# A hand-written order of operations anew: eight chunks of a fused attention and feed-forward kernel

## The chip, the cores and the metric

The kernel runs on 1 core of a Trainium2 chip. The metric is the device time of one execution in microseconds (us), the median of several runs; lower is better.

## The reference

A linear attention (softmax of q over the head's elements, softmax of k over the sequence), and a feed-forward layer with SiLU on its result:

```python
# q, k, v: (8 batches, 8 heads, 576 positions, 64), float32
q_s = softmax(q, axis=-1)                       # over the 64 elements
k_s = softmax(k, axis=2)                        # over the 576 positions
kv  = einsum('bhsd,bhse->bhde', k_s, v)
x   = einsum('bhsd,bhde->bhse', q_s, kv)        # then (4608 tokens, 512)
h   = x @ w_in                                  # (4608, 2048)
out = (h * sigmoid(h)) @ w_out                  # (4608, 512), float32
```

## The kernel before

The 4608 tokens are worked in nine chunks of 512: chunk 0 to chunk 8. Attention is worked per batch (576 positions); its results feed the chunk that holds its tokens. Chunk 0 is done in another form than the rest, with 576 tokens at once ("wide"), and chunk 1 has the 448 tokens that are left of its 512.

The whole program is straight-line. Each piece of work is an operation with a short name, and a string ORDER lists the names; a loop at the end calls them one by one. Each engine (PE, DVE, ACT, POOL, and SP for its DMA orders) executes its own operations in the order in which they stand in that string; between engines there are only semaphores, set from the data and buffers that operations share. So the string fixes five queues, and an operation that has to wait holds up all that stands behind it on its engine. The first operations of batch 0 (loads, softmax, its products, and the first two products of chunk 0) stand ahead of ORDER as plain calls.

The names, as far as the text needs them (b is a batch, c a half of its heads, t a chunk):

- `lqb.c`, `lkb.c`, `lvb.c`: a load of q, k or v (L152), 576 KB. Batches 1 and 2 are loaded from POOL's queue, batches 0 and 3 to 7 from SP's. Each of q, k, v has two buffers, so a load waits until the operation that read the older content is done: `eqb.c` (ACT, Exp of q, L163), `ekb.c` (ACT, Exp of k, L168), `vcb.c` (cast of v). `W1a0` to `W1d` and `W2a` to `W2d` load the weights (L564, L570) from POOL's queue.
- `zb.c` sums the Exp of q (DVE), `nb.c` divides by it (POOL, L216; for batches 0 and half of 1 on DVE). `tqb` is a transpose of q by DMA from SP's queue (L226); for batches 0 and 1 `trb.c` transposes on PE and `tcb.ca`, `tcb.cb` copy the result (ACT, DVE). `kvb` is the product of k and v (PE, L248), `kcb` normalises it (DVE). `Xt.i` (PE, L282; `xt1.i` for chunk 1) makes a chunk's x, `xt.ca` and `xt.cv` copy it from PSUM (ACT or DVE).
- Chunk 0: `wF` is block F of 16 of its first product (PE, L307: 8 matmuls of 128x288, four contraction steps for each of two PSUM banks), `hF` the tanh (ACT, L320), `vF` the rest of SiLU (DVE, L323), `pF` step F of 16 of the second product (PE, L445, four matmuls of 512 columns into PSUM banks 2 to 5). The blocks F use four sets of two banks in turn (4, 2, 0, 6). `po0` to `po3` copy its output, `os0` to `os3` store it.
- Chunks 1 to 8, first product: one level of a seven-product scheme (Strassen-Winograd). `gt.g.i` is product i (PE, L425, 8 matmuls) for half g of the hidden columns, in the order 1 2 6 5 7 4 3, accumulated in two pairs of banks. `st.g.i` copies a partial sum from PSUM (ACT or DVE), `at.g.i` adds another (DVE, L403), `ut.g.i` is SiLU (ACT, L409). `xst.i` and `WSg.i` are the sums of operands (DVE). Half of chunk 1 is done plainly: `m0` to `m7` (PE, L335, banks 0 to 3 in turn), `mu0` to `mu7` its SiLU (ACT, L345).
- Chunks 1 to 8, second product: `bt.i.m` (PE, L503, 8 matmuls; `e` for chunk 8) in the same scheme, with `St.i` and `T1` to `T4` as operand sums (DVE), `sat`, `sbt`, `sct` as partial sums (ACT), `wat`, `wbt`, `wct`, `wlt` as output sums, `ot.m` as stores (SP). The second product of a chunk runs between the first-product steps of the next.
- `gcopy` (ACT) copies 64 tokens' columns of chunk 0's hidden values over to chunk 1. `heat` is PE work without a result.

Exp and SiLU need different function tables on ACT; a change of table is an instruction of its own (ACT_TABLE_LOAD, 1.28 us).

Of the kernel before, what the change touches and what calls it, by code (L numbers as in the profile page):

```python
# [15 lines left out]


ORDER = """
    lk1.0 w1 lk1.1 w2 h1 w0 h2 v1 w3 h0 W2b1 w5 v0 v2 h3 w4 WS0.1 h5 w6 v3 h4 W2b2 v4 w7 v5 w8 h7 h6 v7 w9
    lv1.0 h8 v6 w11 v8 h9 lv1.1 w10 eq1.0.0 v9 h11 WS0.2 w12 eq1.1.0 v11 h10 w13 WS1.1 eq1.0.1 v10 h12 w15  # L20
    qp1a h13 v12 w14 eq1.1.1 v13 qp1b WS1.2 W2c1 p0 h14 z1.0 ek1.0 p1 z1.1.0 n1.0 z1.1.1 p2 h15 ek1.1 v15 p3
    WS1.4 W2c2 tr1.0 v14 lq2.0 p4 tc1.0a tc1.0b lq2.1 n1.1 p5 W2d p6 lk2.0 T1 vc1.0 lk2.1 p7 tr1.1 lv2.0
    vc1.1a vc1.1b gcopy WS1.3 kv1 lv2.1 tc1.1b p8 tc1.1a kc1 WS0.3 xt1.0 xt1.1 x1.0a x1.1v p9 x1.2a x1.3v
    g1.1.1 xs1.1 xs1.2 xs1.4 g1.1.2 s1.1.0a WS0.4 p10 xs1.3 eq2.0 a1.1.0 p11 eq2.1 z2.0 g1.1.6 g1.1.5
    s1.1.1a z2.1 n2.0 p12 ek2.0 g1.1.7 p13 s1.1.2v n2.1 ek2.1 p14 a1.1.2 g1.1.4 p15 tq2 u1.1.4 g1.1.3 po2v
    vc2.1 po1a m0 po3v po0a a1.1.1 u1.1.0 vc2.0 m1 lk3.0 mu0 m2 T2 lq3.0 mu1 lq3.1 m3 u1.1.2 lk3.1 T3 m4
    lv3.0 u1.1.1 lv3.1 m5 T4 mu2 os0 mu4 kv2 mu5 m6 mu3 kc2 X2.0 mu6 X2.1 x2.0v m7 x2.1a x2.3a x2.2v g2.1.1
    mu7 xs2.1 xs2.2 g2.1.2 s2.1.0v b1.1.0 ek3.0 S1.1 g2.1.6 eq3.1 lk4.0 S1.2 b1.2.0 os1 s2.1.1a b1.1.1 xs2.3
    xs2.4 eq3.0 a2.1.0 g2.1.7 vc3.0 sa1 b1.2.1 lq4.0 z3.1 s2.1.2a g2.1.5 vc3.1 ek3.1 b1.6.0 a2.1.2 n3.1
    lk4.1 g2.1.4 z3.0 g2.1.3 u2.1.0 g2.0.2 u2.1.4 wa1 n3.0 b1.6.1 a2.1.1 u2.1.2 g2.0.1 sb1 S1.3 kv3 tq3  # L30
    s2.0.0a b1.5.0 kc3 u2.1.1 S1.4 g2.0.6 b1.7.0 s2.0.1v lv4.0 ek4.1 b1.7.1 lv4.1 a2.0.0 os3 g2.0.7 sc1
    ek4.0 b1.5.1 s2.0.2v g2.0.5 eq4.0 lk5.0 wc1 lq4.1 g2.0.4 a2.0.2 os2 b1.4.0 vc4.0 lk5.1 z4.0 u2.0.4
    g2.0.3 u2.0.2 b1.3.0 lv5.0 vc4.1 a2.0.1 u2.0.0 lq5.0 b1.4.1 n4.0 X3.0 wl1v X3.1 kv4 x3.0a x3.1v x3.2a
    b1.3.1 kc4 x3.3a xs3.1 u2.0.1 g3.1.1 xs3.2 wb1 g3.1.2 s3.1.0a xs3.3 xs3.4 g3.0.2 S2.1 g3.1.6 S2.2 eq4.1
    b2.2.0 s3.1.1a b2.1.0 z4.1 ek5.0 b2.1.1 a3.1.0 g3.1.7 n4.1 sa2 ek5.1 b2.6.0 s3.1.2v g3.1.5 vc5.0 tq4
    g3.1.4 a3.1.2 u3.1.0 b2.6.1 u3.1.4 S2.3 g3.1.3 sb2 lq5.1 g3.0.1 u3.1.2 a3.1.1 lv5.1 lk6.0 b2.7.0 s3.0.0a
    o1.0 S2.4 b2.2.1 u3.1.1 a3.0.0 g3.0.6 lv6.0 b2.7.1 s3.0.1v eq5.0 g3.0.5 wa2 g3.0.7 sc2 lq6.0 z5.0 b2.4.0
    s3.0.2a lk6.1 b2.5.0 vc5.1 eq5.1 a3.0.2 g3.0.4 o1.1 n5.0 z5.1 g3.0.3 u3.0.4 b2.5.1 a3.0.1 n5.1 u3.0.0
    b2.4.1 wc2 u3.0.2 X4.0 X4.1 kv5 x4.1v x4.0a tq5 wl2v b2.3.0 u3.0.1 x4.3v g4.1.1 xs4.1 x4.2a b2.3.1 xs4.2
    s4.1.0a S3.1 g4.1.2 wb2 g4.1.6 lq6.1 a4.1.0 ek6.1 b3.1.0 xs4.3 s4.1.1a b3.1.1 xs4.4 S3.2 ek6.0 g4.1.5  # L40
    g4.1.7 sa3 eq6.0 b3.2.0 s4.1.2v eq6.1 b3.2.1 lq7.0 kc5 lk7.0 b3.6.0 a4.1.2 lv6.1 lq7.1 g4.1.4 o2.0 wa3
    g4.1.3 z6.0 u4.1.4 b3.5.0 u4.1.0 S3.3 g4.0.1 lk7.1 b3.6.1 a4.1.1 s4.0.0a g4.0.2 sb3 u4.1.1 g4.0.6 a4.0.0
    b3.5.1 s4.0.1a S3.4 b3.7.0 vc6.1 u4.1.2 g4.0.7 z6.1 vc6.0 g4.0.5 s4.0.2a b3.7.1 a4.0.2 n6.1 g4.0.4 sc3
    u4.0.2 g4.0.3 wc3 n6.0 b3.3.0 u4.0.4 a4.0.1 b3.4.0 u4.0.0 X5.0 X5.1 kv6 x5.0a x5.1v tq6 x5.3a x5.2v
    b3.3.1 u4.0.1 xs5.1 g5.1.1 xs5.2 wb3 b3.4.1 s5.1.0v o2.1 ek7.1 g5.1.2 kc6 g5.1.6 wl3a xs5.3 xs5.4 a5.1.0
    lv7.0 b4.2.0 s5.1.1a lv7.1 b4.1.0 S4.1 eq7.1 g5.1.7 ek7.0 b4.2.1 s5.1.2v o3.1 g5.1.5 S4.2 b4.1.1 u5.1.0
    a5.1.2 g5.1.4 sa4 g5.0.2 o3.0 u5.1.4 wa4 g5.1.3 S4.3 u5.1.2 vc7.1 g5.0.1 b4.6.0 a5.1.1 vc7.0 s5.0.0a
    b4.6.1 a5.0.0 u5.1.1 g5.0.6 S4.4 b4.5.0 s5.0.1a b4.5.1 sb4 u5.0.0 g5.0.7 g5.0.5 s5.0.2v b4.7.0 eq7.0
    a5.0.2 b4.7.1 z7.1 g5.0.4 sc4 g5.0.3 b4.4.0 a5.0.1 u5.0.4 b4.4.1 wc4 u5.0.1 X6.0 X6.1 kv7 x6.0v u5.0.2
    x6.3v b4.3.0 x6.1a kc7 b4.3.1 x6.2a xs6.1 xs6.2 g6.1.1 xs6.4 wl4v g6.1.2 S5.1 s6.1.0a b5.1.0 a6.1.0  # L50
    g6.1.6 xs6.3 g6.0.2 wb4 s6.1.1a S5.2 b5.1.1 o4.0 b5.2.0 S5.3 g6.1.7 S5.4 b5.2.1 s6.1.2a z7.0 g6.1.5 sa5
    g6.1.4 wa5 n7.0 b5.6.0 a6.1.2 u6.1.4 b5.6.1 g6.0.1 n7.1 sb5 u6.1.0 g6.1.3 s6.0.0a b5.7.0 a6.1.1 tq7
    b5.7.1 a6.0.0 u6.1.1 g6.0.6 sc5 b5.5.0 s6.0.1a o4.1 g6.0.5 u6.1.2 g6.0.7 b5.5.1 s6.0.2v b5.4.0 wc5
    g6.0.4 a6.0.2 b5.4.1 u6.0.4 b5.3.0 u6.0.2 X7.0 X7.1 x7.0a x7.1v g6.0.3 x7.2a xs7.1 u6.0.0 g7.1.1 x7.3v
    a6.0.1 b5.3.1 s7.1.0a xs7.2 g7.1.2 wl5a u6.0.1 g7.1.6 o5.1 a7.1.0 b6.1.0 s7.1.1a xs7.4 xs7.3 g7.1.5 wb5
    g7.1.7 S6.1 o5.0 b6.1.1 s7.1.2a S6.2 g7.0.2 sa6 a7.1.2 u7.1.0 g7.1.4 S6.3 b6.2.0 u7.1.4 g7.1.3 u7.1.2
    g7.0.1 a7.1.1 b6.2.1 s7.0.0a b6.6.0 wa6 u7.1.1 S6.4 g7.0.6 b6.6.1 s7.0.1v b6.5.0 sb6 a7.0.0 g7.0.7
    b6.7.0 s7.0.2a b6.7.1 b6.5.1 sc6 u7.0.0 g7.0.4 wc6 g7.0.5 u7.0.4 b6.4.0 a7.0.2 b6.3.0 X8.0 X8.1 x8.0v
    g7.0.3 x8.2a x8.1v u7.0.2 b6.4.1 xs8.1 a7.0.1 x8.3a g8.1.1 xs8.3 g8.1.2 s8.1.0a xs8.2 b6.3.1 wl6a u7.0.1
    g8.1.6 wb6 b7.1.0 S7.1 o6.0 s8.1.1a b7.2.0 a8.1.0 g8.1.7 o6.1 xs8.4 b7.1.1 S7.2 s8.1.2a g8.1.5 sa7  # L60
    u8.1.0 b7.2.1 a8.1.2 g8.1.4 S7.3 g8.1.3 u8.1.4 g8.0.2 a8.1.1 u8.1.2 g8.0.1 u8.1.1 b7.6.0 s8.0.0v b7.6.1
    wa7 g8.0.6 a8.0.0 sb7 b7.5.0 s8.0.1a S7.4 b7.7.0 g8.0.7 g8.0.5 s8.0.2v b7.7.1 a8.0.2 b7.5.1 sc7 u8.0.0
    g8.0.4 wc7 g8.0.3 u8.0.4 b7.4.0 a8.0.1 u8.0.2 b7.3.0 u8.0.1 b7.3.1 e1.0 wb7 S8.1b e1.1 o7.0 S8.1a b7.4.1
# [7 lines left out]
def kernel(  # L71
# [477 lines left out]
    for name, src in (("qt", q), ("kt", k)):  # L549
        load(0, name, src, 0, nc.sync)  # L550
        if name == "qt":
            load(0, name, src, 1, nc.sync)
    load(0, "vt", v, 0, nc.sync)
    load(0, "kt", k, 1, nc.sync)
    load(0, "vt", v, 1, nc.sync)
# [19 lines left out]
    heat(20)  # L575
    exp_q(0, 0)
    qsum(0, 0)
    exp_q(0, 1)
    nc.gpsimd.tensor_copy(gate, st[0]["kt", 0][0:1, 1, 0:1])
    load_w1(0, 4, 0, 2)  # L580
    load_w1(0, 4, 2, 4)
    load_w1(4, 8)
    load_w1(8, 12)
    load_w1(12, 16)
    load(1, "qt", q, 0, nc.gpsimd)
    load(1, "qt", q, 1, nc.gpsimd)
    load_w2(0, 4)

    qnorm(0, 0, nc.vector)
    qsum(0, 1)  # L590
    exp_k(0, 0)
    tr(0, 0, 0, 5, 0)
    tr(0, 0, 5, J, 1)
    heat(7)
    qnorm(0, 1, nc.vector)
    vcast(0, 0, nc.scalar)
    trcopy(0, 0, 0, 5, 0, nc.scalar)
    trcopy(0, 0, 5, J, 1)
    kv(0, 0)
    kvcopy(0, 0, 1)  # L600
    tr(0, 1, 0, 5, 2)
    tr(0, 1, 5, J, 3)
    exp_k(0, 1)
    xt_mm(0, 0, 0, 320, 4, 0)
    xt_mm(0, 0, 320, 256, 0, 0)
    heat(3, 6)
    vcast(0, 1, nc.scalar, 0, 1)
    vcast(0, 1, nc.vector, 1, 2)
    trcopy(0, 1, 0, 5, 2, nc.scalar)
    trcopy(0, 1, 5, J, 3)  # L610
    kv(0, 1)
    kvcopy(0, 1, 2)
    heat(2, 3)
    xt_evac(0, 0, 4, 0, 320, 0, nc.scalar)
    xt_evac(0, 0, 0, 0, 256, 320, nc.vector)
    xt_mm(0, 1, 0, 320, 6, 0)
    xt_mm(0, 1, 320, 256, 2, 0)
    wide_mm(0, (0, 1))
    xt_evac(0, 1, 6, 0, 320, 0, nc.scalar)
    xt_evac(0, 1, 2, 0, 256, 320, nc.vector)  # L620
    wide_mm(2, (0, 1))
# [217 lines left out]
```

## Time and profile before

| what | value |
|---|---|
| median of 3 runs | 257.55 us (257.51 to 258.29) |
| profiled execution, its own time | 258.61 us |
| its span | 256.6 us |
| PE busy | 249.1 us (97%), 2732 matmuls |
| DVE, ACT, POOL busy | 206.2 us (80%), 190.9 us (74%), 65.8 us (26%) |
| granted TensorE clock | 1.0 throughout |
| DMA | 45.89 MB, of it q1 (issued by SP and ACT) 33.56 MB, q0 (issued by POOL) 11.60 MB |
| chain that ended last | PE 76%, DMA 11%, issue 5%, POOL 3%, ACT 2%, DVE 1% |

The span is the time between the first and the last instruction in one profiled execution; its own time has 2.0 us more around it. The chain that ended last is followed back from the last instruction, at each step to what released it. The span is drawn in 40 slices of 6.4 us; a digit is the busy share of a slice in tenths. "L" numbers are lines of the kernel, and a line can be that of a helper that many operations share. Matmul ends are modelled, so PE counts as busy in small waits too.

### The profile page before, as it was taken

How to read it: one execution, taken by the hardware profiler on the slowest of the kernel's cores; microseconds unless marked ns; L12 is line 12 of the kernel's file. 1: busy time of each engine (PE TensorE's matmuls, PEld its weight loads, DVE VectorE, ACT ScalarE, POOL GpSimd, SP SyncE). 2: the span in 40 equal slices, each digit the busy share in tenths (PEclk: the TensorE clock that was granted, in tenths of full speed). 3: DMA queues.
4: the chain of work that ended last, by engine and by line, in shares of the span. 5: the costliest groups of instructions: out<-in, count | busy, mean ns of one | idle time of the engine just before them, and what ended most of it. 6: DMA issues, size and time to landing. Idle time of an engine off the chain costs nothing.

```text
span 256.6 us, 6459 instructions
## 1 busy us (share of the span) xinstructions
PE 249.1 (97%) x2732; PEld 204.2 (80%) x2732; DVE 206.2 (80%) x276; ACT 190.9 (74%) x225; POOL 65.8 (26%) x62
## 2 busy tenths in 40 slices
PE   8799999999999999999999999999999999999994
...
DMA  7999999979959957996874960021807000600365
GB/s 248 348 181 297 302 301 283 351 140 393 378 128 213 403 187 137 361 335 168 276 266 68 224 236 3 3 52 32 163 14 153 13 0 4 148 18 0 66 141 123
DMA packets 36044, 45.89 MB, mean 179 GB/s; under 512 B 16288, under 2 KB 21088, under 8 KB 36016
## 3 DMA queue, kind: packets, MB, share of 16 engines
q1 hardware_dynamic: 29456, 33.56, 45.5%
q0 software_dynamic: 6160, 11.60, 17.8%
...
## 4 chain that ended last, share of the span: by engine, by line
PE 76%; DMA 11%; issue 5%; POOL 3%; ACT 2%; DVE 1%; ACTq 0%; POOLq 0%
PE PS L503 37%; PE PS L425 33%; DMA qt<-in_q_dram 5%; DMA kt<-in_k_dram 5%; PE PS L335 3%; PE PS L248 2%; PE PS L282 2%; POOL W L564 1%; DMA out_dram<-ow 1%; POOL qt L152 1%; DVE GT L323 1%; ACT L409 0%; POOL W L570 0%; ACT sg L320 0%; ACT GT L409 0%
## 5 line engine op out<-in xcount | busy, mean ns | idle before, releaser
L403 DVE TENSOR_TENSOR h<-PS,h 128x1024 f32<-128x1024 f32 (+1 forms) x45 | 54.2, 1206 | 9.3 <-PE PS L425 7.8
L503 PEld LDWEIGHTS <-GT 128*128 128x128 f16 x512 | 50.1, 98 | 5.9
L425 PEld LDWEIGHTS <-WS 128*128 128x128 f16 x480 | 46.7, 98 | 6.5 <-issue 0.6
L409 ACT ACTIVATE GT<-h 128x1024 f16<-128x1024 f32 (+1 forms) x45 | 46.8, 1051 | 0.9 <-DVE h L403 0.7
L503 PE MATMUL PS<-W,GT 128*128 128x256 f16 x384 | 47.3, 273 | 0.0
L425 PE MATMUL PS<-XS,WS 128*128 128x256 f16 (+1 forms) x360 | 45.0, 272 | 0.0
L142 ACT COPY h<-PS 128x1024 f32<-128x1024 f32 (+1 forms) x31 | 31.1, 1003 | 16.9 <-PE PS L425 15.7
L503 PEld LDWEIGHTS <-S 128*128 128x128 f16 x384 | 37.1, 98 | 4.6
L425 PEld LDWEIGHTS <-W 128*128 128x128 f16 x360 | 35.2, 98 | 4.4
L216 POOL TENSOR_TENSOR eq<-eq,rzq 128x1152 bf16<-128x1152 bf16 x13 | 27.3, 2115 | 37.6 <-DVE rzq L211 36.3
L503 PE MATMUL PS<-T,S 128*128 128x256 f16 x256 | 32.2, 273 | 0.0
L144 POOL CAST vaug<-vt 128x1152 bf16<-128x1152 f32 x12 | 15.8, 1328 | 61.5 <-DMA vt<-in_v_dram 61.4
L425 PE MATMUL PS<-XT,W 128*128 128x256 f16 (+1 forms) x240 | 29.7, 272 | 0.0
L144 DVE COPY h<-PS 128x1024 f32<-128x1024 f32 (+1 forms) x14 | 17.0, 1212 | 9.2 <-PE PS L425 4.4
L207 DVE TENSOR_REDUCE zq<-eq 128x18 f32<-128x1152 bf16 x14 | 18.8, 1342 | 4.1 <-ACT eq L163 4.0
L163 ACT ACTIVATE eq<-qt 128x1152 bf16<-128x1152 f32 (+1 forms) x18 | 18.9, 1055 | 3.1 <-DMA qt<-in_q_dram 2.8
L168 ACT ACTIVATE ek<-kt 128x1152 bf16<-128x1152 f32 x16 | 18.6, 1163 | 3.0 <-DMA kt<-in_k_dram 2.9
...
L409 ACT ACTIVATE GT<-PS 128x1024 f16<-128x1024 f32 (+1 forms) x15 | 15.2, 1013 | 6.1 <-PE PS L425 6.1
L503 PE MATMUL PS<-T,GT 128*128 128x256 f16 x128 | 16.3, 272 | 0.0
L307 PE MATMUL PS<-XT,W 128*128 128x288 f16 x128 | 16.0, 286 | 0.2 <-DMA W<-in_moe_w_in_dram 0.2
L503 PE MATMUL PS<-W,S 128*128 128x256 f16 x128 | 16.1, 273 | 0.0
...
## 6 DMA issues: line engine op xcount, KB each, us to landing
...
```

Of the source, the lines that this page charges most:

```text
L142: eng.copy(out=o, in_=i)
L144: eng.tensor_copy(o, i)
L163: nc.scalar.activation(out=half(st[b]["eq"], cc)[:, :, g0:g1], in_=jgd(b, "qt", cc)[:, :, g0:g1], func=ACT.Exp)
L168: nc.scalar.activation(out=half(ek, cc), in_=jgd(b, "kt", cc), func=ACT.Exp)
L207: nc.vector.reduce_sum(out=z, in_=e, axis=AX.X)
L216: eng.tensor_tensor(out=e, in0=e, in1=r[:, :, :, None].to_broadcast([128, J, 2, D]), op=ALU.mult)
L307: nc.tensor.matmul(out=PS[:, WIDE[fb] + n, 0:S // 2], lhsT=W1[:, c, fb * 128:(fb + 1) * 128], rhs=XTS[0][:, c, n * (S // 2):(n + 1) * (S / ...
L335: nc.tensor.matmul(out=PS[:, bank, o0:TCH], lhsT=W1[:, c, fb * 128:(fb + 1) * 128], rhs=XTS[t % 2][:, c, o0:TCH], start=(c == 0), stop=(c ...
L403: nc.vector.tensor_tensor(out=four(t, i), in0=group_bank(t, g), in1=four(t, i), op=ALU.add)
L409: nc.scalar.activation(out=group_out(t, f, n), in_=x, func=ACT.Silu, scale=1.0 / XS)
L425: nc.tensor.matmul(out=PS[:, bank + p // 2, (p % 2) * HT:(p % 2) * HT + width(t)], lhsT=a[:, c, p * 128:(p + 1) * 128], rhs=bb[:, c, 0:wid ...
L503: nc.tensor.matmul(out=PS[:, bank, m * HN:(m + 1) * HN], lhsT=a[:, fc, m * 128:(m + 1) * 128], rhs=bb[:, fc, :], start=(first and fc == 0) ...
```

## The change

ORDER is replaced from chunk 0's first product to the products of chunk 7; from `u8.1.1 b7.6.0 s8.0.0v` on it is word for word the same. The plain calls ahead of it become operations and stand at its head, in the order that they had, but for one swap (`x0.1v` ahead of `x0.1a`; the two are on different engines). Each block `wF` becomes two operations: `wF.0` does the contraction steps 0 and 1 for both of its banks, `wF.1` the steps 2 and 3. No operation's own work changes apart from that, nor the engine on which it runs.

The start of the string before (the calls ahead of it ended in `w0`'s and `w2`'s first halves):

```
    lk1.0 w1 lk1.1 w2 h1 w0 h2 v1 w3 h0 W2b1 w5 v0 v2 h3 w4 WS0.1 h5 w6 v3 h4 W2b2 v4 w7 v5 w8 h7 h6 v7 w9
    lv1.0 h8 v6 w11 v8 h9 lv1.1 w10 eq1.0.0 v9 h11 WS0.2 w12 eq1.1.0 v11 h10 w13 WS1.1 eq1.0.1 v10 h12 w15
    qp1a h13 v12 w14 eq1.1.1 v13 qp1b WS1.2 W2c1 p0 h14 z1.0 ek1.0 p1 z1.1.0 n1.0 z1.1.1 p2 h15 ek1.1 v15 p3
    WS1.4 W2c2 tr1.0 v14 lq2.0 p4 tc1.0a tc1.0b lq2.1 n1.1 p5 W2d p6 lk2.0 T1 vc1.0 lk2.1 p7 tr1.1 lv2.0
    vc1.1a vc1.1b gcopy WS1.3 kv1 lv2.1 tc1.1b p8 tc1.1a kc1 WS0.3 xt1.0 xt1.1 x1.0a x1.1v p9 x1.2a x1.3v
    g1.1.1 xs1.1 xs1.2 xs1.4 g1.1.2 s1.1.0a WS0.4 p10 xs1.3 eq2.0 a1.1.0 p11 eq2.1 z2.0 g1.1.6 g1.1.5
    s1.1.1a z2.1 n2.0 p12 ek2.0 g1.1.7 p13 s1.1.2v n2.1 ek2.1 p14 a1.1.2 g1.1.4 p15 tq2 u1.1.4 g1.1.3 po2v
    vc2.1 po1a m0 po3v po0a a1.1.1 u1.1.0 vc2.0 m1 lk3.0 mu0 m2 T2 lq3.0 mu1 lq3.1 m3 u1.1.2 lk3.1 T3 m4
    lv3.0 u1.1.1 lv3.1 m5 T4 mu2 os0 mu4 kv2 mu5 m6 mu3 kc2 X2.0 mu6 X2.1 x2.0v m7 x2.1a x2.3a x2.2v g2.1.1
    ...
    s2.0.0a b1.5.0 kc3 u2.1.1 S1.4 g2.0.6 b1.7.0 s2.0.1v lv4.0 ek4.1 b1.7.1 lv4.1 a2.0.0 os3 g2.0.7 sc1
    ek4.0 b1.5.1 s2.0.2v g2.0.5 eq4.0 lk5.0 wc1 lq4.1 g2.0.4 a2.0.2 os2 b1.4.0 vc4.0 lk5.1 z4.0 u2.0.4
    g2.0.3 u2.0.2 b1.3.0 lv5.0 vc4.1 a2.0.1 u2.0.0 lq5.0 b1.4.1 n4.0 X3.0 wl1v X3.1 kv4 x3.0a x3.1v x3.2a
    b1.3.1 kc4 x3.3a xs3.1 u2.0.1 g3.1.1 xs3.2 wb1 g3.1.2 s3.1.0a xs3.3 xs3.4 g3.0.2 S2.1 g3.1.6 S2.2 eq4.1
```

and after:

```
    lq0.0 lq0.1 lk0.0 lv0.0 lk0.1 lv0.1 heat0 eq0.0 z0.0 eq0.1 gate W1a0 W1a1 W1b W1c W1d lq1.0 lq1.1 W2a n0.0 z0.1
    ek0.0 tr0.0 heat1 n0.1 vc0.0 tc0.0a tc0.0b kv0.0 kc0.0 tr0.1 ek0.1 X0.0 heat2 vc0.1a vc0.1b tc0.1a tc0.1b kv0.1
    kc0.1 heat3 x0.0a x0.0v X0.1 w0.0 x0.1v x0.1a w2.0 w1.0 w1.1 w0.1 h1 h0 lv1.0 w2.1 v1 h2 w3.0 w3.1 w5.0 v0 w5.1
    v2 w4.0 h3 w4.1 v3 w6.0 h4 h5 v4 w6.1 h6 v5 w7.0 w7.1 w8.0 h7 w8.1 v6 h8 W2b1 w9.0 w9.1 v7 v8 w11.0 w10.0 WS0.3
    h9 lk1.1 eq1.0.1 WS0.1 v9 w10.1 eq1.0.0 w11.1 w12.0 h10 W2b2 w12.1 h11 v10 lk1.0 qp1a lv1.1 h12 w13.0 v11 v12
    w13.1 w14.0 eq1.1.1 h13 W2c1 w15.0 w14.1 w15.1 v13 WS1.1 qp1b z1.0 eq1.1.0 p0 p1 vc1.0 p2 h14 z1.1.0 h15 p3
    WS1.3 v14 lq2.1 n1.0 ek1.1 z1.1.1 v15 p4 n1.1 p5 ek1.0 W2c2 lq2.0 p6 T1 tr1.0 tc1.0a p7 lk2.0 tr1.1 vc1.1a W2d
    tc1.0b vc1.1b kv1 tc1.1b tc1.1a kc1 p8 xt1.0 xt1.1 WS1.2 p9 x1.0a x1.2a x1.1v g1.1.1 x1.3v xs1.1 xs1.3 WS1.4
    eq2.1 g1.1.2 s1.1.0a p10 lk2.1 xs1.2 g1.1.6 p11 a1.1.0 eq2.0 s1.1.1a g1.1.5 g1.1.7 xs1.4 gcopy lv2.0 ek2.0 p12
    p13 z2.1 lv2.1 p14 z2.0 s1.1.2v lq3.0 ek2.1 a1.1.2 g1.1.4 u1.1.4 g1.1.3 T3 p15 T2 u1.1.0 po0a m1 a1.1.1 po1a
    n2.1 m0 m2 mu1 lk3.0 u1.1.1 n2.0 vc2.1 m5 mu0 m3 m4 WS0.2 u1.1.2 vc2.0 mu3 mu2 kv2 lk3.1 mu4 po2v T4 WS0.4 po3v
    mu5 tq2 kc2 m6 X2.0 X2.1 mu6 x2.1a x2.0v m7 lq3.1 x2.3a mu7 g2.1.1 os2 b1.1.0 x2.2v xs2.1 xs2.3 xs2.2 g2.1.2
    ...
    g2.0.1 g2.1.3 sb1 b1.7.0 os1 s2.0.0a n3.0 wa1 lv4.1 lk4.1 b1.7.1 a2.1.1 a2.0.0 g2.0.6 kv3 lq4.1 u2.1.2 u2.1.1
    lk4.0 s2.0.1v sc1 u2.0.0 b1.5.0 g2.0.7 lv4.0 kc3 tq3 vc4.1 os0 S1.4 ek4.0 g2.0.5 b1.4.0 b1.5.1 s2.0.2v a2.0.2
    g2.0.4 g2.0.3 b1.4.1 wc1 vc4.0 eq4.0 ek4.1 u2.0.4 z4.0 b1.3.1 a2.0.1 u2.0.2 X3.0 x3.1v X3.1 kv4 wl1v S2.1 x3.0a
    g3.1.1 xs3.1 b1.3.0 x3.2a wb1 b2.1.0 u2.0.1 x3.3a n4.0 xs3.3 s3.1.0a g3.1.2 xs3.2 S2.2 eq4.1 a3.1.0 g3.1.6
```

The definition of the blocks:

```diff
     for fb in range(NFB):
-        op(f"w{fb}", wide_mm, fb, range(2 if fb in (0, 2) else 0, NC))
+        op(f"w{fb}.0", wide_mm, fb, (0, 1))
+        op(f"w{fb}.1", wide_mm, fb, (2, 3))
```

158 lines of the change are left out of this document (57 added, 101 removed).

## The prediction

> **What bounds the kernel now.** I read the page's head and slices first, then a table of windows, then the chain of waits in order of time, then the timelines of PE, POOL and SP.
>
> The slices and the windows say where time can be won at all (columns after the window: its length, then each engine's busy time with its instructions, clock, DMA share, GB/s):
>
> ```profile
> span 256.6 us, 6459 instructions
> PE   8799999999999999999999999999999999999994
> DMA  7999999979959957996874960021807000600365
> ```
> ```profile
> 14.60:31.00 16.40, 16.21 (x136) 12.59 (x137) 12.82 (x20) 11.33 (x19) 6.27 (x9) 1.00 1.17 276
> 31.00:54.10 23.10, 22.12 (x220) 13.28 (x218) 21.18 (x36) 16.80 (x20) 12.97 (x13) 1.00 1.00 281
> 54.10:120.00 65.90, 65.87 (x868) 55.58 (x868) 61.73 (x78) 64.36 (x75) 22.95 (x14) 1.00 0.89 273
> 120.00:236.00 116.00, 116.00 (x1229) 102.73 (x1228) 91.12 (x110) 82.95 (x95) 13.69 (x8) 1.00 0.36 93
> ```
>
> From 54.1 to 236 us PE idles 0.03 us; from 236 on the order is the same in both kernels. All idle PE time that a new order could remove lies in 14.6 to 54.1: 0.19 + 0.98 = 1.17 us (0.5%). In that stretch the DMA engines are at their limit (share 1.0 and more).
>
> The chain of waits in order of time (start, us, what) says what ends that stretch. (Landings here and below: the last of a load's 16 semaphore updates in the trace.)
>
> ```profile
> 38.30 12.31 DMA kt<-in_k_dram
> 50.61 0.02 issue
> ...
> 50.73 1.14 issue
> 51.87 1.28 ACT L409
> ...
> 53.16 0.93 ACT GT L409
> 54.09 0.04 issue
> 54.13 4.70 PE PS L335 x24
> ```
>
> Load lk2.1 lands at 50.61; then come ek2.1 (Exp of it, 1.16), the table load for Silu, u1.1.4 (0.92), which frees PSUM bank 0, and at 54.13 m0. The PE timeline shows two waits there, for load W2d before p12 and for u1.1.4 before m0:
>
> ```profile
> 47.62 1.02 PE L445 MATMUL PS<-W,GT 128*128 128x512 f16 x4 [0.30 <-DMA W<-in_moe_w_out_dram]
> 54.13 2.05 PE L335 MATMUL PS<-XT,W 128*128 128x448 f16 x10 [0.60 <-ACT GT L409]
> ```
>
> So the first 54 us are a queue of loads, the rest is a PE at its limit. I judge the change by two questions: when does lk2.1 land, and does PE get a new wait after the m steps.
>
> **Part 1, the halves of chunk 0.** Before, w1 does four matmuls per bank over the whole contraction: after 10 matmuls from 14.96 PE waits 0.19 us for W1a1. After, w1.0 has two matmuls more that need only W1a0: about 2 x 0.122 = 0.24 us earlier. But w5 needs W1b, which lands at 19.10, and w5 started at 19.26: at most 0.12 us is left. The count of matmuls is the same (128); the halves by themselves do nearly nothing. p0 waits for v13 (the last reader of bank 2); with three Exp halves ahead of h13 in both orders I lay it out to end near 30.8 (before 30.96).
>
> **Part 2, what stands before kv1.** Before, tr1.0 waits 0.28 us for n1.0 (POOL, to 34.69); after, three more p steps stand ahead of it (3 x 0.865 us), so that wait goes. What is late next is kv1: it needs ek1.0, and lk1.0 is now behind lv1.0, W2b1, lk1.1 and W2b2. That set of loads is the one that was complete at 36.53 before, so ek1.0 runs 36.6 to 37.8, then tc1.0a (0.68) and vc1.1a (0.67) on ACT: kv1 at about 39.2, as before (39.31). Gain 0.1, kept only if nothing later binds.
>
> **Part 3, p12.** W2d moves behind lk2.0. The loads through W2d are now those that were through lk2.0 before: 49.09 instead of 47.58. p12 is moved behind g1.1.7 (0.77 us), so PE reaches it near 48.2 to 48.5 and waits 0.6 to 0.9, against 0.30 before. With p12 to p14, g1.1.4, g1.1.3 and p15 after it (4 x 0.865 + 2 x 0.77 = 5.0 us) PE reaches the first m step at 54.1 to 54.2: by itself no change.
>
> **Part 4, SP's queue: the term that decides.** Before, SP's first order after its prologue is the transpose tq2, which needs n2.0 and n2.1, and it holds SP back:
>
> ```profile
> 51.68 3.35 SPq L226 DMA_TRANSPOSE qT<-eq  x1
> 55.22 0.43 SPq L152 DMA_DIRECT2D kt<-in_k_dram  x1
> 55.76 0.92 SPq L152 DMA_DIRECT2D qt<-in_q_dram  x2
> ```
>
> So all loads of batch 3 start after POOL's queue has nearly drained. After, lq3.0, lk3.0 and lk3.1 stand ahead of tq2. lq3.0 needs only the buffer that eq2.1 frees (a load waits for the first of two freed buffers: before, lq4.0 was issued at 66.57, between the end of eq3.1 at 65.97 and that of eq3.0 at 67.93). eq2.1 now comes first and its load lands near 40.6; behind x1.2a (to 42.4) it ends near 43.5. lq3.0 is issued there, and its packets come about 1.3 us later, near 44.9, when W2d, lk2.0, lk2.1, lv2.0 and lv2.1 are still queued.
>
> Its price: one such load alone takes 1.47 us of all engines (lq0.0 and lq0.1 landed at 4.36 and 5.83). Bounds: 0, if POOL's older orders all go first; 1.47, if it is through before lk2.1. The nearest row is 10.8 to 12.5 us, where the last SP load of the prologue and POOL's first W1 load had packets under way together: the SP load landed 1.46 us after the one before it, not slowed. I take 1.47.
>
> [...]
>
> Then lk2.1 lands at 52.1 and W2d at 50.55. Both paths move alike: 52.1 + 1.16 + 1.28 + 0.92 + small waits gives the first m step at 55.6; W2d + 5.05 gives 55.6 too. lk3.0 follows when ek2.0 is done (near 50.0) and its packets meet the last of lk2.1: 0 to 0.5 us, I take 0.15 (its packets should start near 51.3, and only the last of the 16 shares of lk2.1 is open by then). gcopy (1.04 us on ACT) moves to just before ek2.0, where ACT waits for a load anyway; without that cover it would cost up to 1.04. kv2 needs lv2.1, 54.07 before, near 57 now, with two casts of 1.16 (2.15 beside DVE copies): ready 59.4 to 60.4, and PE comes to it at 60.2: nothing or 0.2, inside the range.
>
> **Part 5, chunks 1 to 7.** PE has no slack to give, so a new order can only add waits. I went through each wait by the PE work that lies between its cause and its user. Most keep their distance. The tight one is at X3. ACT now does u2.0.0 (1.05) ahead of the Exp block, so u2.0.4, which frees bank 0 for X3.0, comes 0.95 later, while PE has one product (0.87) less between g2.0.4 and X3.0: the slack of 1.8 us (84.45 to 86.24) is gone. And b1.3.1 no longer lies between kv4 and g3.1.1: x3.0a ended 1.08 before g3.1.1, and 0.87 of that cover leaves. Bounds 0 and 0.55, I take 0.2. ACT's table loads are 15 after the first in both orders; no cost. m5 waits for mu1, which has u1.1.0 and two copies ahead of it: 0.1, counted in the upper bound.
>
> **Sum.** +1.47 + 0.15 + 0.2 = +1.8 us; the gains of parts 1 to 3 are 0, since lk2.1 ends the stretch. The profiled execution has 256.6 us of span and 258.61 in all (2.0 around it), 1.06 above the median of the runs; its own time would become 260.4, the median 257.55 + 1.8 = 259.4.
>
> **Rivals.**
> - *The extra load hides (no change).* If POOL's orders go first, lq3.0 costs nothing, and lk2.1 lands at 50.6: the first m step at 54.1 to 54.3, X3 at 0 to 0.5, hence 257.5 to 258.2. For it: POOL's descriptors are older. Against: the row at 10.8 to 12.5. Chance 0.18.
> - *The loads run better (faster).* lq2.1 landed 3.77 us after lq2.0, where 1.5 is usual, because the share of one engine of the 16 came last (the 15th share at 43.63, the 16th at 45.68); that lag stays with every later load. If the new order escapes it, lk2.1 lands up to 2.2 earlier. It decides from a landing of lk2.1 before 49.8 on; PE then binds, and the gain ends at the 1.17 us of idle: 256.4 to 256.8. Against: the same bytes go through the same engines, and lq3.0 must be paid first. Chance 0.11.
> - *More falls in (slower still).* lk3.0 shares fully (0.5), X3 costs 0.55, kv2 and m5 0.3, lv2.1 late: 1.47 + 1.35 + 0.5 for a further wait behind them gives 260.9. Chance 0.1.
> - *Forecast* (258.6 to 260.3): 0.61.
>
> About 0.3% (0.8 us) is what a measurement of this kernel can tell from no change. Faster 0.11, same 0.18, slower 0.71. The range takes in the no-change case and most of the slower one: 257.0 to 260.9.
>
> **What would show it.** In the profile after, the step m1 at 55.6 (54.1 to 54.3 if the load hides, below 53.4 if the loads run better); the first SP load after the prologue issued near 43.6 and POOL's last kt load landing near 52.1; PE waiting about 2 us in total ahead of p12 and m1; PE busy without gaps from there to 236 but for some tenths at X3 (L282, L425, near 87 to 89). The forecast is wrong if lk2.1 lands at 51 or earlier, or if PE's idle time after 60 us exceeds 0.8.

## Result: 3.3% slower, and the profile after

| | before | after |
|---|---|---|
| median (4 runs each) | 257.53 us (257.23 to 258.29) | 266.16 us (264.75 to 267.75) |
| profiled execution, its span | 258.61, 256.6 us | 267.75, 266.0 us |
| PE, DVE, POOL busy | 249.1, 206.2, 65.8 us | 252.1, 210.4, 68.7 us |

The ratio is 1.0332 (95% interval 1.0264 to 1.0401). I had forecast 259.4 us and a range up to 260.9: the sign was right, the size was not, and the time lies well outside the range. An execution more than 1.5% above the fastest of its kernel is left out of the times and ratios below; in a_pool, a_pool2 and a_all_kv1 the profiled execution was such a one, so these three have no profile here.

The head and slices of the profile after. One slice of PE is only three tenths busy, and in that slice and the next the granted clock is 0.7:

```profile
span 266.0 us, 6471 instructions
PE   8799999999999399999999998999999999999994
PEclk9999999999999779999999999999999999999999
DMA  7999999999499917879991880038000700420265
```

The same windows as before (length, then busy time of PE, PEld, DVE, ACT, POOL with instructions, clock, DMA share, GB/s). The front has not become worse (PE 22.36 us where 22.12 stood); 5.6 us of idle time lie in 54.1 to 120, where there were 0.03, and 1.0 behind 120:

```profile
31.00:54.10 23.10, 22.36 (x221) 13.63 (x220) 22.40 (x34) 17.35 (x21) 12.31 (x12) 1.00 1.09 344
54.10:120.00 65.90, 60.28 (x719) 50.04 (x716) 55.15 (x70) 56.28 (x65) 22.82 (x14) 0.95 0.79 225
120.00:236.00 116.00, 114.97 (x1291) 101.10 (x1290) 93.15 (x115) 85.30 (x97) 16.19 (x9) 1.00 0.44 107
```

PE's waits behind 60 us (for what; us in total, times, longest): one wait has most of it, X3.0 (L282) for bank 0, which u2.0.4 frees.

```profile
PE PS L282 <- ACT GT L409: 5.1, 1, 5.1
PE PS L503 <- DVE GT L477: 0.9, 1, 0.9
PE PS L425 <- ACT h L142: 0.5, 1, 0.5
PE PS L425 <- DVE h L403: 0.2, 1, 0.2
```

The chain of waits ahead of X3.0 (start, us, what), to be set beside the chain of before that ended in lk2.1 and m0:

```profile
76.68 9.70 DMA qT<-eq
...
86.46 0.04 ACT eq L163
...
87.53 1.15 ACT ek L168
...
88.69 1.28 ACT L409
...
89.99 1.03 ACT GT L409
...
91.06 1.01 PE PS L282 x12
```

The transpose tq3 takes 9.7 us from issue to landing. eq4.0 overwrites the buffer that tq3 reads, so it starts at 86.46, just after the landing at 86.38; on ACT, in its order, ek4.1, the table load and u2.0.4 stand behind eq4.0, and PE stands behind u2.0.4. In before tq3 was issued at 74.93, landed at 80.20, and eq4.0 started at 80.97, with 0.8 us to spare.

SP's rows say why tq3 is late (start, us on SP, operation):

```profile
64.87 2.00 SPq L441 DMA_DIRECT2D out_dram<-ow  x2
70.46 0.37 SPq L152 DMA_DIRECT2D vt<-in_v_dram  x1
70.93 0.41 SPq L152 DMA_DIRECT2D kt<-in_k_dram  x1
71.44 0.42 SPq L152 DMA_DIRECT2D qt<-in_q_dram  x1
71.91 0.53 SPq L152 DMA_DIRECT2D kt<-in_k_dram  x1
74.61 0.37 SPq L152 DMA_DIRECT2D vt<-in_v_dram  x1
76.68 5.57 SPq L226 DMA_TRANSPOSE qT<-eq  x1
```

SP's loads and transpose in before, and ACT's eq4.0 there (SP's stores of output are left out):

```profile
64.94 0.38 SPq L152 DMA_DIRECT2D kt<-in_k_dram  x1
66.57 0.56 SPq L152 DMA_DIRECT2D qt<-in_q_dram  x1
70.41 0.37 SPq L152 DMA_DIRECT2D kt<-in_k_dram  x1
74.93 3.24 SPq L226 DMA_TRANSPOSE qT<-eq  x1
...
80.97 1.15 ACT L163 ACTIVATE eq<-qt 128x1152 bf16<-128x1152 f32 x1
```

In after nothing is issued from 66.87 to 70.46: the next order is lv4.1, whose buffer comes free when vc3.1 is done. Then five loads go out just ahead of tq3, on the queue that tq3 uses, and the last of them, lv4.0, lands at 82.19. In before three loads stood there (lk4.0, lq4.0, lk4.1); they began at 64.94 and were all landed at 74.14, before tq3 was issued.

After X3's wait PE runs at half its clock (granted clock 0.50 from 90.08 to 96.90 us). The windows around it:

```profile
86.00:90.00 4.00, 0.00 (x0) 0.00 (x0) 2.24 (x3) 3.51 (x4) 0.48 (x1) 1.00 0.90 280
90.00:91.00 1.00, 0.00 (x0) 0.00 (x0) 0.46 (x1) 1.00 (x2) 1.00 (x1) 0.54 0.83 279
95.00:97.00 2.00, 2.00 (x11) 1.40 (x10) 0.31 (x1) 1.98 (x2) 0.00 (x0) 0.52 0.00 0
97.00:99.00 2.00, 2.00 (x21) 1.78 (x19) 2.00 (x4) 1.46 (x2) 0.00 (x0) 1.00 0.00 0
```

X3, kv4 and the next three products took 6.49 us (91.06 to 97.55). At clock 1 they take 0.63 + 0.77 (a_tq3_first, rows below) + 3 x 0.87 (a product in before's chain) = 4.0: 2.5 us lost to the clock.

Account of the 9.4 us between the two profiled spans: X3's wait 5.1, the clock 2.5, b4.7.1, g3.0.4 and g4.0.3 together 1.6 (0.9 + 0.5 + 0.2), kv1 0.75 (shown below); less the 0.9 us that before's execution waited ahead of p12 and m0. That is 9.05.

This is the account of one execution of after, the slowest of four. Two of the four (267.75 and 266.90 us) had a mean granted clock of 0.987, which is what 6.8 us at half clock make of a span of 266; the other two (264.75 and 265.42) had 0.997 and 1.0, so little or nothing of the slow stretch. The pairs lie 2.2 us apart, near the 2.5 above; the faster pair is still over 7 us slower than before.

### The profile page after: what moved, and what is told of

Its sections match the earlier page's. It is cut to its first block, busy times and chain, and to the rows that moved or that the text cites. A ratio compares the mean times of both kernels' runs of the same rounds, so it can differ in the third digit from the quotient of the medians.

```text
span 266.0 us, 6471 instructions
## 1 busy us (share of the span) xinstructions
PE 252.1 (95%) x2732; PEld 206.2 (78%) x2732; DVE 210.4 (79%) x276; ACT 191.1 (72%) x225; POOL 68.7 (26%) x62
## 4 chain that ended last, share of the span: by engine, by line
PE 63%; DVE 13%; DMA 10%; ACT 7%; issue 3%; SPq 1%; POOL 1%; ACTq 0%; DVEq 0%; POOLq 0%
PE PS L503 26%; PE PS L425 24%; DMA qT<-eq 6%; PE PS L307 5%; DMA vt<-in_v_dram 4%; DVE h L403 3%; PE PS L445 3%; DVE zq L207 2%; PE PS L335 2%; PE PS L282 2%; PE PS L248 2%; ACT eq L163 2%; DVE GT L477 1%; ACT ek L168 1%; DVE WS L373 1%
## 5 line engine op out<-in xcount | busy, mean ns | idle before, releaser
L503 PE MATMUL PS<-W,GT 128*128 128x256 f16 x384 | 48.2, 273 | 0.9 <-DVE GT L477 0.9
L216 POOL TENSOR_TENSOR eq<-eq,rzq 128x1152 bf16<-128x1152 bf16 x13 | 29.4, 2265 | 53.4 <-DVE rzq L211 49.6
L503 PEld LDWEIGHTS <-S 128*128 128x128 f16 x384 | 37.7, 99 | 5.1 <-issue 0.2
L425 PE MATMUL PS<-XT,W 128*128 128x256 f16 (+1 forms) x240 | 30.9, 276 | 0.0
L144 POOL CAST vaug<-vt 128x1152 bf16<-128x1152 f32 x12 | 17.1, 1431 | 27.1 <-DMA vt<-in_v_dram 16.1
L144 DVE CAST XT<-PS 128x512 f16<-128x512 f32 (+1 forms) x17 | 11.0, 678 | 7.4 <-PE PS L282 7.3
L503 PE MATMUL PS<-W,S 128*128 128x256 f16 x128 | 16.8, 282 | 0.0
```

What stands on the lines that cost most here:

```text
L144: eng.tensor_copy(o, i)
L216: eng.tensor_tensor(out=e, in0=e, in1=r[:, :, :, None].to_broadcast([128, J, 2, D]), op=ALU.mult)
L425: nc.tensor.matmul(out=PS[:, bank + p // 2, (p % 2) * HT:(p % 2) * HT + width(t)], lhsT=a[:, c, p * 128:(p + 1) * 128], rhs=bb[:, c, 0:wid ...
L503: nc.tensor.matmul(out=PS[:, bank, m * HN:(m + 1) * HN], lhsT=a[:, fc, m * 128:(m + 1) * 128], rhs=bb[:, fc, :], start=(first and fc == 0) ...
```

## Experiments

Each edit but two only changes places in ORDER (b_halves splits the blocks of chunk 0, a_heat adds work to PE); each time is the median, each ratio that to the kernel before in the same batch of runs.

**f_after, f_before: which part of the order.** The string is cut at g2.1.1, the first product of chunk 2.

```diff
 f_after:  after's ORDER up to g2.1.1, the rest in before's order
 f_before: before's ORDER up to g2.1.1, the rest in after's order
```

> The changed order up to g2.1.1 (chunk 0, chunk 1, batch 3's first loads), and from there the order before for all that is left. If the loss lies behind that point (the chain z3.0, n3.0, tq3, eq4.0 and later ones), this kernel costs nothing or gains up to 0.6 us: 256.7 to 258.0. Rival (the front carries a loss, since three loads stand ahead of tq2 there too): eq3.0 or eq3.1 waits for tq2, PE waits in chunk 2, 258.5 to 261 us.

> The order before up to g2.1.1, and from there the changed order for all that is left. If the loss lies behind that point: 262.5 to 267 us, with PE waiting at X3.0 for u2.0.4. Rival (the front's shift in time makes the later waits): 257.5 to 260 us.

f_after: 259.43 us, ratio 1.0086 (1.0068 to 1.0104). f_before: 265.52 us, 1.0298 (1.0252 to 1.0345), with a wait of 3.3 us at X3, behind a tq3 that took 8.1 us (77.16 to 85.30), and half the clock from 91.0 to 94.4. So some 8 us lie behind the cut and 2 ahead of it; the later part does not need the new front.

**b_halves: the halves of chunk 0 alone.**

```diff
-  w1
+  w1.0 w1.1      (every block, both halves next to each other, in before's order; the first halves of w0 and w2 stay ahead of ORDER)
```

> The kernel before with nothing changed but the blocks of chunk 0 in halves of the contraction (each block's two halves directly behind one another). By part 1 of the prediction: w1.1 0.2 us earlier, at most 0.12 left at w5, nothing at the first m step; 257.0 to 257.6 us, no change. Rival (the early start is kept): 0.3 us or more faster at the first m step and in all.

257.16 us, 0.9991 (0.9979 to 1.0004): no change.

**a_tq3_first and b_loads_ahead: the loads ahead of tq3.**

```diff
 a_tq3_first (after):
-  lv4.1 lk4.1 ... lq4.1 ... lk4.0 ... lv4.0 kc3 tq3
+  lk4.1 ... lk4.0 ... kc3 tq3 lv4.1 lv4.0 lq4.1
 b_loads_ahead (before):
-  lk4.0 ... lq4.0 ... lk4.1 ... tq3 ... lv4.0 ... lv4.1 ... lq4.1
+  lk4.0 ... lq4.0 ... lk4.1 lv4.0 lv4.1 lq4.1 tq3
```

> The changed order with lv4.1, lv4.0 and lq4.1 moved behind tq3 in SP's queue; nothing else. Queue theory (tq3 came late because five loads of batch 4 stood ahead of it on the same queue, and eq4.0, which overwrites what tq3 reads, held up ACT): tq3 lands at 80.5 to 82.5 instead of 86.38, X3.0 starts at 86.3 to 87.3 instead of 91.06, the TensorE clock stays at 1.0, and the time falls by 6 to 7.5 us to 258.7 to 260.2. Rival (POOL's later n3.0 and the late loads of batch 4 as such are the cause): the wait only moves to kv4 or ek4.0, X3.0 at 89 or later, 263 to 265 us.

> The kernel before with lv4.0, lv4.1 and lq4.1 moved ahead of tq3 in SP's queue; nothing else. Queue theory: tq3 is issued at about 75 as before, but lands at 83 to 85 instead of 80.19, eq4.0 waits for it, X3.0 starts 2 to 4 us late, and the time is 259.5 to 262. Rival (loads ahead of a transpose cost nothing): within 0.8 us of 257.5.

a_tq3_first: 263.29 us, 1.0227 (1.0209 to 1.0245). tq3 lands 4.6 us after its issue; X3.0's wait for u2.0.4 is down to 0.4 us, and no slice around it has a clock under 0.9 (0.7 in after). So the theory's chain is gone at X3. But of after's 8.6 us only 2.9 are gone, and the time lies in the range that was on record for the rival: kv4 now waits for lv4.x, and tq3 is issued at 78.22, still later than before's 74.93. PE's rows there:

```profile
87.54 0.63 PE L281 MATMUL PS<-qT,kvn 64*64 64x192 bf16 x16 [0.39 <-ACT GT L408]
89.07 0.77 PE L247 MATMUL PS<-vaug,ek 64*64 64x65 bf16 x72 [0.90 <-POOL vaug L143]
```

b_loads_ahead: 258.42 us, 1.0047 (1.0026 to 1.0069), between the two theories: tq3 took 7.3 us instead of 5.3 and landed at 80.91; eq4.0 waited 1.5 us for it and started at 81.02, but PE did not wait at X3.0, where before has the slack of 1.8 us that part 5 of the prediction reads.

**a_heat: the clock.** After, with PE kept busy by 24 matmuls without a result ahead of X3.0.

```diff
+  op("hx", heat, 24, 6)      # in ORDER: ... u2.0.2 hx X3.0 ...
```

> The changed order with 24 matmuls without a result (128x512, into bank 6) ahead of X3.0; it stands where PE idled for 5.1 us. Clock theory (the idle time itself brings the granted clock down to 0.5 for about 6 us afterwards, which costs some 2.6 us): X3.0 still starts near 91, the clock stays at 1.0, the time falls by 2 to 2.7 us to 263.4 to 264.2. Rival (the dip has another cause, such as the load on the chip at that place): clock dips as before, 266 us.

267.23 us, 1.0375 (1.0325 to 1.0426). The clock stayed at 1.0 from 85 to 99 us, with PE busy for 13.7 of these 14 us; the half clock was seen only where PE had idled (after, f_before). The time did not fall: the work took 5.34 us from 88.92, past u2.0.4, and X3.0 came at 94.19; u2.0.4 had been done at 88.7, so PE would hardly have idled here without the added work either, and that idling is the cause stays likely, not proved. In this execution, with the same order ahead of the added work, tq3 took only 4.7 us (79.36 to 84.04), and PE had lost some 2 us in five smaller waits between 58 and 87. So where the loss falls differs between executions. Nor does the run show the price of the slow stretch; for that there are only the 2.5 us of the account and the 2.2 us between after's executions.

**a_pool, a_pool2: the order on POOL and DVE.** a_tq3_first with two more moves that take effect (the two kernels are the same; lv3.0's move in the string leaves SP's order as it was).

```diff
-  vc3.1 n3.1 vc3.0        S1.3 ... z3.0
+  vc3.0 vc3.1 n3.1        z3.0 S1.3
```

> The changed order with the three loads behind tq3 (as in a_tq3_first), and also vc3.0 ahead of vc3.1 on POOL (with lv3.0 ahead of os2) and z3.0 ahead of S1.3 on DVE, as they stood before. Theory (each step of the chain z3.0, n3.0, tq3, eq4.0, table, u2.0.4 is late by the work put ahead of it): n3.0 ends by 75 instead of 78.2, tq3 lands at 78 to 80.5, X3.0 needs no wait of over 0.3 us, 261.0 to 262.3 us, the rest of the loss being the waits at kv4, g3.0.4, g4.0.3 and b4.7.1. Rival (POOL and DVE are not on that path): 263.3 us as a_tq3_first.

> After, with lv4.1, lv4.0 and lq4.1 behind tq3 on SP's queue, and also lv3.0 and vc3.0 back ahead of lv3.1 and vc3.1, and z3.0 ahead of the sum S1.3 on DVE. Theory (the whole wait at X3 comes from tq3, half from the loads on its queue, half from n3.0 being late through POOL's and DVE's order): n3.0 starts about 1.5 us earlier than with the loads alone moved, X3.0 follows the work before it with no gap over 0.5 us, kv4 keeps a wait of about 1 us for lv4.x, and the time is 260 to 262 us, against 263.3 with the loads alone. Rival (what is left is in later chunks and POOL's and DVE's order costs nothing): 263 us again.

a_pool gave one time, 261.74 us, and no interval: inconclusive. a_pool2: 262.15 us (median of four), 1.0176 (1.0148 to 1.0204), about 1 us below a_tq3_first. So POOL's and DVE's order is worth about 1 us more, as the theory had it, though a little above its range; with no profile of it, where that 1 us was won is not shown.

**b_both: loads and POOL/DVE order put into before.**

```diff
-  lk4.1 ... tq3 ... lv4.0 lv4.1 ... lq4.1      vc3.0 vc3.1      z3.0 ... S1.3
+  lk4.1 lv4.0 lv4.1 lq4.1 tq3                  vc3.1 vc3.0      S1.3 z3.0
```

> Before, with both halves of what makes tq3 late put in: lv4.0, lv4.1 and lq4.1 ahead of tq3 on SP's queue (alone 258.4 us), the cast vc3.1 ahead of vc3.0 on POOL and the sum S1.3 ahead of z3.0 on DVE. Theory (the two add up, and before has little slack: eq4.0 starts 0.8 us after tq3 lands): n3.0 ends 2 us later, tq3 lands near 83, X3.0 has a gap of 1 to 3 us, and the time is 260 to 262 us. Rival (in before's order the lateness is slack, the loss at X3 needs the other moves of the new order too): 258 to 259 us.

257.84 us (median of eight), 1.0018 (0.9999 to 1.0037): the rival holds. In the profiled execution tq3 was issued at 74.90 and landed at 80.68, with eq4.0 at 80.78. Something else in after had to make these moves cost 5 us. Two more executions took 261.5 us at a mean clock of 0.99; neither was profiled, so whether the wait at X3 came back in them is open.

**a_lv41, b_lv41: one load.** The candidate was lv4.1, which holds SP in after until vc3.1 is done.

```diff
 a_lv41 (after):   -  lv4.1 lk4.1 ... tq3        +  lk4.1 ... tq3 lv4.1
 b_lv41 (b_both):  -  lk4.0 ... lv4.1 ... tq3    +  lv4.1 lk4.0 ... tq3
```

> After, with the load lv4.1 alone moved behind tq3 on SP's queue. In after lv4.1 waited at the head of SP from 66.87 to 70.46 us for vc3.1, and the four loads behind it were issued from 70.9 to 74.6 and landed up to 82.19, 5.5 us after tq3 had been issued. Theory (it is this wait that puts the loads in front of tq3): the loads behind it are issued from about 67 us, lv4.0 waits for vc3.0 as before and lands before 80, tq3 lands 4 to 5 us after the later of its issue and that landing, X3.0 has a gap of 0.5 to 2.5 us, no stretch at half clock, and the time is 263 to 264.5 us. Rival (the number of loads ahead of tq3 counts, not the wait): X3.0 keeps a gap over 3.5 us and the time is 265.5 us or more.

> Before with the three moves that gave 257.95 us (lv4.x and lq4.1 ahead of tq3, vc3.1 ahead of vc3.0, S1.3 ahead of z3.0), and lv4.1 now ahead of lk4.0, so that SP waits with it for vc3.1 as in after. Theory: the loads of batch 4 start about 5 us later, near 69 us, the last of them lands near 82, tq3 near 85 to 86, X3.0 has a gap of 2 to 4 us with a stretch at half clock behind it, and the time is 261 to 264 us. Rival (slack of before's order covers this too): 258 to 259 us.

a_lv41: 263.45 us, 1.0227 (1.0151 to 1.0302), as much as moving three loads (the interval overlaps a little with after's; the profile is the firmer evidence). SP's rows: the loads behind lv4.1 now go out from 65.92, and all have landed before tq3 is issued (lv4.0 at 76.72):

```profile
65.92 0.54 SPq L151 DMA_DIRECT2D kt<-in_k_dram  x1
68.36 0.37 SPq L151 DMA_DIRECT2D qt<-in_q_dram  x1
68.78 0.46 SPq L151 DMA_DIRECT2D kt<-in_k_dram  x1
69.35 0.41 SPq L151 DMA_DIRECT2D vt<-in_v_dram  x1
77.42 2.81 SPq L225 DMA_TRANSPOSE qT<-eq  x1
```

tq3 landed at 82.02, 4.6 us after its issue, and the mean clock of that execution was 1.0. b_lv41: 261.53 us, 1.0153 (1.0081 to 1.0226), some 3.5 us above b_both and inside the theory's range. tq3 took 7.45 us and landed at 84.51, about as expected; but that the time fitted is luck: it was lost a step earlier, at kv3, where PE waited 2.5 us, so that X3.0 then came late by itself and had a gap of 0.3, in an execution with a mean clock of 0.999. What lv4.1's wait costs alone in before's order is so not shown. Why kv3 waited, three rows (one of DVE, one of POOL, one of PE) tell:

```profile
70.03 3.19 DVE L473 TENSOR_TENSOR GT<-GT 128x2048 f16<-128x2048 f16 x1
...
70.01 2.12 POOL L212 TENSOR_TENSOR eq<-eq,rzq 128x1152 bf16<-128x1152 bf16 x1
...
76.50 0.81 PE L244 MATMUL PS<-vaug,ek 64*64 64x65 bf16 x72 [2.48 <-DVE h L399]
```

S1.3, a sum of 1.22 us, began 0.02 us behind n3.1 on POOL and took 3.19, longer by nearly all of n3.1's 2.12 us; all that stood behind it on DVE, down to the addition that frees kv3's bank, came late. In b_both S1.3 began at 69.56, 0.15 us ahead of n3.1, and took 1.26: a few tenths of a us decide who waits.

**a_all: the small gaps.** a_pool2 with two more moves. In after, S4.3 (DVE, 160.96) took 2.34 us while POOL worked on n7.0 and n7.1, and b4.7.1 waited for it.

```diff
-  lk6.0 lv5.0 tq4          z7.0 ... S4.3
+  tq4 lv5.0 lk6.0          S4.3 z7.0
```

> As a_pool2, with two more moves: lv5.0 and lk6.0 behind tq4 on SP's queue, and the sum S4.3 ahead of z7.0 on DVE. In after S4.3 ran while POOL worked on n7.0 and took 2.34 us instead of 1.22, and the block b4.7.1 waited 1.1 us for it; g3.0.4 waited 0.7 us behind tq4. Theory (the small gaps too come from moved steps that meet another engine's work): both gaps go and the time is 1.5 to 2 us below a_pool2, 258 to 260 us. Rival (the waits move to the next steps, S4.4 and n7.x): no more than 0.5 us below a_pool2.

260.69 us, 1.0121 (1.0079 to 1.0164), 1.5 us below a_pool2, with intervals that overlap, and above the theory's 258 to 260. Only half of the theory held: b4.7.1 has no gap; g3.0.4 still has 0.7 us, tq4 taking 6.4 us.

**b_lq3_ahead, f_lq3: the loads of batch 3 ahead of tq2**, part 4 of the prediction.

```diff
 b_lq3_ahead (before):  -  tq2 ... lk3.0 ... lq3.0 ... lk3.1   +  lq3.0 lk3.0 lk3.1 tq2
 f_lq3 (f_after):       -  lq3.0 ... lk3.0 ... lk3.1 ... tq2    +  tq2 lq3.0 lk3.0 lk3.1
```

> The kernel before with lq3.0, lk3.0 and lk3.1 moved ahead of tq2 in SP's queue; nothing else. By part 4 of the prediction lq3.0, issued near 45.4, takes 1.47 us from POOL's loads: lk2.1 lands at 51.5 to 52.2 instead of 50.61, the first m step starts at 55 or later, 258.7 to 259.4 us. By the rival that the first profile after suggests (such a load's packets start over 3 us after its issue and then share with the last loads only): lk2.1 at 50.4 to 51, the first m step at 54.0 to 54.4, 257.2 to 258.1 us.

> After's order up to the first product of chunk 2 and before's order from there (259.43 us), with the loads lq3.0, lk3.0 and lk3.1 moved back behind tq2. Theory (the 2 us that the front of the new order costs are those loads, as they cost 2.7 us in the order of before): 257 to 257.8 us, with no gap at g2.1.7 and tq2 landing near 57. Rival (the 2 us are a collision: in that kernel the casts vc3.0 and vc3.1 on POOL ran from 64.4 to 68.4 us beside DVE's S1.2 and xs2.3, which took 2.06 and 1.37 us instead of 1.22 and 0.42; that depends on when DVE gets to them, not on the loads): 259 us again.

b_lq3_ahead: 260.0 us, 1.0113 (1.0077 to 1.0148): the three loads cost 2.7 us in before's order, but not where I had put it: lk2.1 landed at 51.03 (50.61 before), while lv2.1 came at 55.74 and tq2 at 61.08 (54.07 and 56.34), kv2 waited 0.8 us for the cast of lv2.1 and g2.1.7 1.6. That second wait is in part the meeting of DVE and POOL again: there S1.2 took 2.06 us and xs2.3 1.37 beside a cast (1.22 and 0.42 in b_halves, ahead of its first cast). f_lq3: 259.23 us, 1.0065 (1.0038 to 1.0092), not apart from f_after: in the new front the loads are not the 2 us.

**f_kv1, f_kv1_xs, a_all_kv1: what the front costs.** In every kernel with the new front kv1 stops twice. PE's rows in after (in brackets the wait before it and its releaser):

```profile
38.88 0.22 PE L248 MATMUL PS<-vaug,ek 64*64 64x65 bf16 x2
39.66 0.47 PE L248 MATMUL PS<-vaug,ek 64*64 64x65 bf16 x35 [0.56 <-DVE qT L144]
40.32 0.48 PE L248 MATMUL PS<-vaug,ek 64*64 64x65 bf16 x35 [0.19 <-DVE vaug L144]
```

T1 (1.22 us on DVE from 38.05) now stands ahead of tc1.0b, which kv1 needs; in before tc1.0b stood ahead of T1.

```diff
 f_kv1 (f_after), a_all_kv1 (a_all):  -  T1 tr1.0 ... tc1.0b vc1.1b    +  tr1.0 ... tc1.0b vc1.1b T1
 f_kv1_xs (f_kv1):                    -  S1.1 ... S1.2 ... xs2.3 xs2.4  +  xs2.3 xs2.4 S1.1 ... S1.2
```

> After's order up to the first product of chunk 2 and before's order from there (259.43 us), with T1 behind tc1.0b and vc1.1b on DVE. In every kernel with the new front kv1 stops for 0.56 and 0.19 us, because T1 (1.22 us) stands ahead of the copies tc1.0b and vc1.1b on DVE; with the old front it does not. Theory (0.75 us of the front's 2 us is this order on DVE): kv1 runs without a stop, and the time is 0.5 to 0.8 us lower, 258.6 to 258.9 us. Rival (T1's later end is paid at p8 to p12, or the 0.75 us is slack for the loads of W2d): 259.3 to 259.6 us.

> As f_kv1, and xs2.3 and xs2.4 also ahead of the sums S1.1 and S1.2 on DVE. In the run of after's front with before's rest, g2.1.7 waited 1.9 us for xs2.3, which stood behind S1.1 and S1.2 while POOL worked on the casts vc3.0 and vc3.1 and S1.2 and xs2.3 took 2.06 and 1.37 us instead of 1.22 and 0.42. Theory (that meeting of DVE and POOL is the rest of the front's cost): g2.1.7 has no gap, the two long instructions are elsewhere or gone, and the time is 257.0 to 257.6 us, within 0.2 us of before. Rival (the wait moves to b1.2.0, which needs S1.2, or to z3.1): 258.3 us or more.

> The mended version of after (260.69 us) with T1 behind tc1.0b and vc1.1b on DVE as well. Theory: 0.5 to 0.8 us less than that, 259.9 to 260.2 us; what then stays over the time of before is the waits at g2.1.3, g3.0.4, g4.0.3 and g5.0.7 (2.4 us in sum in that profile). Rival (the time is won in the front and lost again at chunk 2's first products): 260.7 us.

f_kv1: 259.10 us, 1.0057 (1.0031 to 1.0083); the intervals overlap with f_after's. kv1 runs through, but xt1.0 then has a gap of 0.4 us, for tc1.1b and kc1, which it needs, now stand behind T1: the rival's wait, with a time between the two theories. f_kv1_xs: 259.10 us, 1.0062 (1.0036 to 1.0089); g2.1.7's gap is gone and g2.1.5 has one of 1.25 us: the rival again. a_all_kv1: 260.0 us (median of eight), 1.0096 (1.0068 to 1.0123), as the theory had it, but not apart from a_all. The other piece of the front's cost, g2.1.7 in f_after, reads as the meeting of DVE with POOL once more: the sums S1.1 and S1.2, then xs2.3, beside the casts vc3.0 and vc3.1. DVE's rows and POOL's row in f_after:

```profile
64.02 1.22 DVE L476 TENSOR_TENSOR S<-GT 128x2048 f16<-128x2048 f16 x1
65.27 2.06 DVE L476 TENSOR_TENSOR S<-S,GT 128x2048 f16<-128x2048 f16 x1
67.25 1.37 DVE L382 TENSOR_TENSOR XS<-XT 128x512 f16<-128x512 f16 x1
...
64.40 3.95 POOL L143 CAST vaug<-vt 128x1152 bf16<-128x1152 f32 x2 [6.82 <-DMA vt<-in_v_dram]
```

In b_halves the first cast came at 66.28, when DVE was past these sums, and took 1.16.

With the loads put back (f_lq3) a cast met xs2.4 instead (1.37 us from 66.87). The place of the loss is shown, and that no single move tried here wins it back; what would is open.

Set in a row, the ratios to before fall from 1.0332 (after) to 1.0227 (a_tq3_first), 1.0176 (a_pool2), 1.0121 (a_all) and 1.0096 (a_all_kv1): about 2.7, 1.3, 1.4 and 0.6 us won, of which the last two are not clear of the noise. About 2.5 us stay; the front alone costs some 1.5 to 2 (f_kv1, f_after). No version with the new order beat the kernel before; the best with its back part is a_all_kv1 at 260.0 us.

## Why the prediction was right in sign and wrong in size

- **Bound of the gain.** I took the 0.98 us of waits in 31 to 54 us as something an order could win. They belong to that execution: in b_halves, before's order with no such wait, m0 started at 52.68 instead of 54.13 and the median was the same.
- **Part 1** held: the halves are worth nothing.
- **Part 2** had kv1's start right (38.88; forecast 39.2) and missed what happens inside it. I priced ACT's copies and not the new place of T1 on DVE: 0.75 us.
- **Part 3** had PE at p12 at 48.2 to 48.5 (it came at 48.63). The wait of 0.6 to 0.9 did not come: W2d landed at 47.17, not 49.09. So the first m step came at 53.62, not at 55.6, between the marks of the two rivals.
- **Part 4, the deciding term of 1.47 us, failed where I put it.** lq3.0 was issued at 44.18 (forecast 43.6), but its packets came from 47.66, 3.5 us later and not 1.3, and lk2.1 landed at 48.97 instead of 52.1 (the prediction's other condition for being wrong, 51 or earlier, was met too). Nor is 48.97 a gain of the new order: in b_halves, b_both and b_loads_ahead, which have before's front, lk2.1 landed at 48.8 to 49.2, so the 50.61 that I started from was a late sample. The rival "the extra load hides" was right for this place, though for another reason than the one given: the load did not stand back behind POOL's older orders to the end, it began late. From 48 to 51 us POOL's queue (the rest of lk2.1, then lv2.x) and SP's (lq3.0, then lk3.0 too) shared the engines about half and half, with shares of 0.54 and 0.52. The price of loads ahead of tq2 is real (2.7 us in b_lq3_ahead, where tq2 took 8.0 us), but kv2 and g2.1.7 pay it, and I had no term for tq2 at all.
- **Part 5 is the step that failed most.** "Most keep their distance" and 0.2 us at X3 stood for the some 8 us that f_before shows for this part of the order; in the profile after X3.0 waited 5.1 us, and the half clock behind it cost 2.5. X3 was the right place, u2.0.4 and bank 0 the right wait. But I measured the slack by PE's and ACT's work alone. I did not follow eq4.0 back to tq3 through their common buffer, nor tq3 through SP's queue, where lv4.1 waits for POOL's vc3.1, now ahead of vc3.0, with lv3.1 landing at 68.43. That this wait is the cause at X3 is shown by a_lv41: with lv4.1 alone moved, tq3 took 4.6 us and X3's long wait and the slow clock were gone. The time came down by 2.7 us only, with other waits in its place (0.9 us at kv4 among them), so the 8 us have no single cause, and what is left of them is followed only as far as the experiments go. The prediction's own condition for being wrong (PE idle over 0.8 us after 60) was met with 6.65 us (5.62 + 1.03).
- **A term that I did not have:** sums on DVE beside POOL's work. In before one such sum was lengthened behind 60 us (1.75 us at 74.23); in after six, to 1.47 to 2.34 us; the others took 1.16 to 1.23. S1.3 ahead of z3.0 (2.17 us) helped to make tq3 late, S4.3 (2.34 us) made b4.7.1 wait.
- **The rivals.** "More falls in" was the closest and too small, as it only summed the bounds of waits already named. The stretch at half clock, 2.5 us behind a wait of 5.1, stood in none.
